# Two row tiles issued behind a memset at the start, and one query product and two sets of row statistics placed elsewhere in layer 3

## The chip, the cores and the metric

The kernel runs on one core of a Trainium2 chip. The metric is the device time of one execution in microseconds (us), as the median over runs. The engines are TensorE (PE; its weight loads are listed as PEld), VectorE (DVE), ScalarE (ACT), GpSimd (POOL) and SyncE (SP); SP, ACT and POOL can each issue DMAs.

## The reference

The input is 2048 rows (tokens) of 576 numbers. Four layers follow each other: A, B, A, B, each with a layer norm in front and a residual sum behind.

```python
def _A_ref(x, wqkv, wo):            # H = 32 heads of 18
    q, k, v = ...                   # from x @ wqkv
    phi = lambda t: jnp.where(t > 0, t + 1, jnp.exp(t)) + 1e-6
    pq, pk = phi(q), phi(k)
    kv = jnp.einsum("bhsd,bhse->bhde", pk, v)
    z = jnp.einsum("bhsd->bhd", pk)
    num = jnp.einsum("bhqd,bhde->bhqe", pq, kv)
    den = jnp.einsum("bhqd,bhd->bhq", pq, z)[..., None] + 1e-6
    o = num / den
    return (...)(o, 0, 2, 1, 3).reshape(B, S, D) @ wo

def _B_ref(x, w1, b1, w2, b2):      # 576 -> 4608 -> 576
    y = _layernorm(x, axis=-1)
    h = _gelu(jnp.einsum("bsd,df->bsf", y, w1) + b1)
    return jnp.einsum("bsf,fd->bsd", h, w2) + b2

x = x + _A_ref(_layernorm(x, axis=-1), A_wqkv, A_wo)
x = x + _B_ref(_layernorm(x, axis=-1), B_w1, B_b1, B_w2, B_b2)
x = x + _A_ref(_layernorm(x, axis=-1), A_wqkv, A_wo)
x = x + _B_ref(_layernorm(x, axis=-1), B_w1, B_b1, B_w2, B_b2)
```

(The reference calls `_B_ref` with the norm outside and inside; the kernel folds the two into one, which is why the variance step of a B layer has the form `var * (1 + eps) + eps^2`.)

## The kernel before

**Tiling.** The 2048 rows are 16 tiles of 128 (`NT`), in four column blocks of 512 tokens (`NCB`, `NCA`; `TPC` = 4 tiles each). Between layers the rows lie in DRAM (`x_d`); a layer works on `yT`, the normalised rows turned, so that features are on partitions. Weights stay on the chip. In the code layers are numbered from 0 (`li`): "layer 3" is the third one, `li == 2`, the second A layer.

**Order.** The kernel is written in a framework that records instructions in program order, derives waits from the data, and then lets a scheduler put the instructions of each engine into one fixed queue, by program order and by when they would be ready. `add_manual_dep(..., NOSYNC, ...)` adds an order between two instructions without a semaphore. TensorE's matmuls are chained one behind the other in program order (`pe`, line 138), so TensorE's order is that of the code.

**Start.** Lines 160 to 171 issue the loads: row tile 0 by SP, tiles 1 and 2 by ACT (`by_act=True`), and the others, the key, value and query weights between them, by SP in one chain. ACT's two have a manual order behind the load of the activation table (`table`). POOL meanwhile writes the identity for the transposes (a memset and an `affine_select`, lines 48 and 49), constants, a `pow` that warms up (line 55), and ones and zeros in `v_ring` (lines 183 to 185). TensorE runs nine matmuls on a zeroed tile (`warm_pe`, line 178). Tile 0 is then normalised: two `bn_stats` and an aggregate on VectorE (lines 355 to 362), the variance step (369), the `pow` on POOL (378), the normalisation on VectorE (399), five transposes on TensorE (427), copies into `yT` (430, 431), and the key product (546). Tile 1's statistics are ordered behind tile 0's variance step, its aggregate behind tile 0's normalisation.

**Layer norm pipe.** `LNPipe` takes a row tile by `feed` and moves it one stage further at each `tick`. `hold` is the number of ticks that it waits first. `stats` chooses the engine of the statistics: "dve" for `bn_stats` on VectorE, "act" for two activations with accumulators on ScalarE (lines 337 and 346) and one small step on POOL (348). `after="sum"` orders the statistics behind the latest residual sum, `after="rden"` behind the latest reciprocal denominators. `tp_at` is the row tile of the output projection from which the transposes may come.

**Output projection of an A layer.** The queries' products run in 20 pieces (`q_proj`, group of heads `g` and block `c`), kept in the list `q_left`. In layer 3 sixteen of them run between the key products (line 688), one in front of the first denominators, and two more with their phi deferred (`late`). One is left, of group 4 and block 3. The loop over `t` (line 864) then runs for each row tile `wo_stage(t)`: ten matmuls into a pair of banks (`accA` and `accB` in turn), the residual sum on VectorE (line 524), and the store; for the first four row tiles it feeds the pipe of the following layer. Between them stand, for the next block, `den_stage` (denominators), `quarter_stage` (broadcasts of their reciprocals, copied by ScalarE, line 812), `quarter_scale` (line 818) and `scale_stage` (line 797), which scale the queries on VectorE, and `quad_stage` (line 779). The rest of `q_left` is taken at `t` of 0 and 2, behind all that (line 885). The pipe ticks twice per row tile up to `t` of 9, then once.

All products other than the projection's use four banks in turn (`ps_h`, tag "h").

## Time and profile before

| | us |
|---|---|
| median of 3 runs (lowest to highest) | 764.54 (764.22 to 764.82) |
| profiled execution | 764.51 |
| its span, first to last instruction | 762.8 |
| ACT busy in the span | 336.1 |
| VectorE busy in the span | 271.5 |
| longest groups of TensorE: second product of the B layers (L1013) | 274.8 |
| first product of the B layers (L955, four groups) | 434.0 summed |

The busy times of one engine's groups can overlap, since matmuls are pipelined. The mean granted TensorE clock is given as 1.000. The stages follow one another in the span like this: the first A layer up to 105 us, the first B layer up to 387, layer 3 up to 478, and the last B layer to the end. Lines of the timeline and of the chain of waits begin with start and length in us; in the timeline they go on with engine, line, operation, what is written from what, the shape and the count, and in brackets the idle time before and what ended it. The chain is followed back from the last instruction: each piece is what released the next one.

### The profile page before, as it was taken

Reading aid. Unit: us, or ns where it says so; the run is one execution under the profiler, and the core shown is the slowest. Engines: PE = TensorE matmul, PEld = TensorE weight load, DVE = VectorE, ACT = ScalarE, POOL = GpSimd, SP = SyncE. Lnnn points to the kernel's source line nnn. Section 1 sums busy time; section 2 is a strip of 40 time slices with the busy share of each in tenths; the row PEclk is TensorE's granted clock in tenths of the full one; section 3 lists DMA queues with packets and bytes.
Section 4 is the critical chain, followed back from the end, with each engine's and each line's share of the span. In section 5 each row is a group of like instructions: output and inputs, shape, how many; then the busy total and the mean of one; then the engine's idle time right before and its main releaser. Section 6 shows DMA issues by size and latency. Waiting matters only on the chain.

```text
span 762.8 us, 15788 instructions
## 1 busy us (share of the span) xinstructions
PE 757.0 (99%) x6594; PEld 491.0 (64%) x6594; DVE 271.5 (36%) x684; ACT 336.1 (44%) x750; POOL 125.3 (16%) x198
## 2 busy tenths in 40 slices
PE   8999999999999999999999999999999999999998
PEld 5777664675477457646777767447745754674476
DVE  7786963136023503401355678600240032000000
ACT  5888857204610750264056567560164037205600
POOL 4681241002000301200110005300020021001000
PEclk9999999999999999999999999999999999999999
DMA  9991483016402721330256007530240033011000
GB/s 281 271 282 47 160 277 82 16 48 187 100 25 74 182 72 45 100 79 11 69 133 199 1 22 258 188 83 16 69 110 28 16 126 82 9 32 56 1 9 24
DMA packets 80289, 73.82 MB, mean 97 GB/s; under 512 B 36698, under 2 KB 64858, under 8 KB 80218
## 3 DMA queue, kind: packets, MB, share of 16 engines
q1 hardware_dynamic: 79930, 72.53, 32.3%
q8 instruction: 51, 0.84, 0.5%
q10 hardware_dynamic: 288, 0.30, 0.1%
q14 instruction: 20, 0.16, 0.1%
HBM read 48.03 MB, written 24.77 MB: 95 GB/s over the span
## 4 chain that ended last, share of the span: by engine, by line
PE 97%; DVE 2%; DMA 0%; issue 0%; ACT 0%; ACTq 0%
PE m_ps L1013 36%; PE h_ps L955 20%; PE hp_ps L955 16%; PE q_ps L594 6%; PE wo_ps L828 4%; PE k_ps L546 3%; PE k_ps L618 3%; PE k_ps L635 2%; PE v_ps L567 1%; PE m_half L1013 1%; PE v_ps L564 1%; PE tp L427 1%; PE kvacc L588 1%; PE k_tail L635 1%; DVE xo L524 0%; DMA x<-in_A_x_dram 0%
## 5 line engine op out<-in xcount | busy, mean ns | idle before, releaser
L1013 PE MATMUL m_ps<-w_sb,hT 128*128 128x288 bf16 x2232 | 274.8, 286 | 0.0
L1013 PEld LDWEIGHTS <-hT 128*128 128x128 bf16 x2304 | 224.8, 98 | 59.8 <-issue 3.4
L955 PEld LDWEIGHTS <-w_sb 64*128 64x128 bf16 x2304 | 124.5, 94 | 136.5 <-issue 1.9
L955 PE MATMUL hp_ps<-yT,w_sb 64*128 64x512 bf16 x1152 | 178.0, 376 | 0.0
L955 PE MATMUL h_ps<-yT,w_sb 64*128 64x512 bf16 x1152 | 147.9, 376 | 0.0
L960 ACT COPY relay_sb<-relay_sb 128x1 f32<-128x1 f32 x144 | 28.6, 198 | 259.8 <-PE h_ps L955 217.6
L951 ACT ACTIVATE hT<-h_ps,b1T 128x512 bf16<-128x512 f32 x144 | 91.2, 684 | 44.4 <-PE h_ps L955 44.4
L378 POOL TENSOR_TENSOR ln_rstd<-ln_u,neg_half 128x1 f32<-128x1 f32 x64 | 36.1, 566 | 407.0 <-DVE ln_u L369 227.2
L951 ACT ACTIVATE hT<-hp_ps,b1T 128x512 bf16<-128x512 f32 x144 | 91.2, 693 | 0.0
L524 DVE TENSOR_TENSOR xbf<-m_ps,xo 128x576 bf16<-128x576 f32 x15 | 11.4, 758 | 214.1 <-PE m_ps L1013 214.1
L524 DVE TENSOR_TENSOR xo<-m_ps,xo 128x576 f32<-128x576 f32 x16 | 12.1, 758 | 174.9 <-PE m_ps L1013 174.9
L507 POOL TENSOR_TENSOR xo<-xo,b_bc 128x576 f32<-128x576 f32 x32 | 40.7, 1277 | 100.3 <-DMA xo<-x_d 60.1
L955 PE MATMUL h_ps<-yT,w_tail 64*128 64x512 bf16 x144 | 54.1, 376 | 0.0
L955 PE MATMUL hp_ps<-yT,w_tail 64*128 64x512 bf16 x144 | 54.1, 376 | 0.0
L594 PE MATMUL q_ps<-yT,wqkv_sb 128*126 128x512 bf16 (+1 forms) x200 | 49.7, 381 | 0.0
L828 PE MATMUL wo_ps<-kvwo,pq 126*128 126x288 bf16 (+1 forms) x320 | 44.0, 286 | 0.5 <-DVE xo L524 0.3
L955 PEld LDWEIGHTS <-w_tail 64*128 64x128 bf16 x288 | 27.1, 94 | 17.1
L828 PEld LDWEIGHTS <-pq 126*128 126x128 bf16 (+1 forms) x320 | 29.7, 97 | 10.2 <-DVE pq L797 0.9
L471 ACT ACTIVATE phi_e<-k_ps 128x288 bf16<-128x288 f32 x46 | 19.3, 419 | 38.2 <-PE k_ps L618 35.8
L594 PEld LDWEIGHTS <-wqkv_sb 128*126 128x126 bf16 (+1 forms) x200 | 24.8, 131 | 11.6
L471 ACT ACTIVATE phi_e<-q_ps 126x512 bf16<-126x512 f32 (+1 forms) x40 | 23.9, 597 | 17.4 <-PE q_ps L594 17.4
L479 DVE TENSOR_SCALAR phi_e<-phi_e 128x288 bf16<-128x288 bf16 (+2 forms) x86 | 24.7, 287 | 19.1 <-ACT phi_e L471 18.4
(140 smaller groups left out, 655.6 us busy)
## 6 DMA issues: line engine op xcount, KB each, us to landing
xo<-x_d SPq DMA_DIRECT2D x48, 288.0 KB
x_d<-xo SPq DMA_DIRECT2D x32, 288.0 KB
xl<-x_d SPq DMA_DIRECT2D x24, 288.0 KB
y_d<-turned SPq DMA_DIRECT2D x40, 144.0 KB
w_sb<-in_B_w_dram SPq DMA_DIRECT2D x6, 864.0 KB
yT<-y_d SPq DMA_DIRECT2D x10, 512.0 KB
w_sb<-in_B_w_dram SPq DMA_DIRECT2D x9, 512.0 KB
x_d<-xn SPq DMA_DIRECT2D x16, 288.0 KB
```

Of the source, the lines that this page charges most:

```text
L378: nc.gpsimd.tensor_tensor(out=rstd[:], in0=it["u"][:], in1=neg_half[:], op=ALU.pow)
L471: exp = nc.scalar.activation(out=e_out, in_=ps_ap, func=ACT.Exp)
L479: low = nc.vector.tensor_scalar(out=e[0:rows, 0:n], in0=e[0:rows, 0:n], scalar1=1.0, scalar2=1e-6, op0=ALU.min, op1=ALU.add)
L507: nc.gpsimd.tensor_tensor(out=xo[:], in0=xo[:], in1=b2_bc[:], op=ALU.add)
L524: total = nc.vector.tensor_tensor(out=xn[:, cols].rearrange("p (h n) -> p h n", h=2), in0=halves, in1=xo[:, cols].rearrange("p (h n) -> p ...
L594: pe(nc.tensor.matmul(qp[0:GR[g], :], lhsT=wqkv_sb[:, k, GO[g]:GO[g] + GR[g]], rhs=yT[:, k, c * CA:(c + 1) * CA], start=(k == 0), stop=(k ...
L635: pe(nc.tensor.matmul(dst, lhsT=lhsT, rhs=pk, start=(t == 0), stop=(t == NT - 1)))
L828: pe(nc.tensor.matmul(wp[:, half, 0:HALF], lhsT=pq[(g, c)][0:GR[g], j * P:(j + 1) * P], rhs=kvwo[g][0:GR[g], half * HALF:(half + 1) * HALF ...
L951: act_last["gelu"] = nc.scalar.activation(out=to, in_=ps, func=ACT.Gelu_apprx_tanh, bias=b1T[:, f:f + 1], scale=1.0).ins.name
L955: mm = pe(nc.tensor.matmul(dst[n], lhsT=wt, rhs=mv, start=(seen[n] == 0), stop=(seen[n] == 8)))
L960: relay = nc.scalar.copy(out=relay_sb[:, 1:2], in_=relay_sb[:, 0:1])
L1013: pe(nc.tensor.matmul(acc[half][:, 0:HALF], lhsT=hT[f][:, j * P:(j + 1) * P], rhs=w2_sb[:, f, half * HALF:(half + 1) * HALF], start=(f == ...
```

## The change

Three things. At the start, tile 1's buffer gets a memset of one column by POOL, ordered behind the identity's `affine_select`; ACT's DMA of tile 1 writes the same buffer and so has to wait for it; tile 2's DMA is ordered behind tile 1's, and the order behind the table load is gone. In layer 3, the last query product is taken in front of `wo_stage(0)` and no longer behind it. And the statistics of that layer's first four new row tiles, which feed the last layer, are given out anew: tile 0 on VectorE and tile 1 on ScalarE as before, tile 2 on ScalarE and tile 3 on VectorE (they had it the other way round), with `hold` 6 and 8 where it was 2 and 4. For the first layer (`li == 0`) the expressions give what they gave.

```diff
-        nc.gpsimd.affine_select(out=ident[:], in_=ident[:], compare_op=ALU.not_equal, fill=1.0,
+        ident_done = nc.gpsimd.affine_select(out=ident[:], in_=ident[:], compare_op=ALU.not_equal, fill=1.0,
                                 base=0, pattern=[[-1, P]], channel_multiplier=1)
...
             if by_act:
+                if t == 1:
+                    tag = nc.gpsimd.memset(x0[:, 0:1], 0.0)
+                    tc.add_manual_dep(tag.ins, ident_done.ins.name, NOSYNC, reason="second rows behind the first")
                 load = nc.scalar.dma_start(out=x0[:], in_=x_in[t * P:(t + 1) * P, :])
-                tc.add_manual_dep(load.ins, table.ins.name, NOSYNC, reason="table first")
+                if t == 2:
+                    tc.add_manual_dep(load.ins, chain["act"], NOSYNC, reason="start-up DMA issue order")
+                chain["act"] = load.ins.name
...
-        table = nc.scalar.preload_act_table_set("natural_log_exp_and_others")
+        nc.scalar.preload_act_table_set("natural_log_exp_and_others")
...
                 if xn is not None and next_kind == "B" and t < TPC:
-                    lnp.feed(xn, t, "B", "pool", "act", hold=(2, 2, 2, 4)[t] if li > 0 else (2, 8, 8, 10)[t], tp_at=6 + 2 * t if li > 0 else (6, 10, 11, 14)[t],
-                             **(dict(after="sum") if t % 2 == 0 else dict(stats="act", after="rden")))
+                    lnp.feed(xn, t, "B", "pool", "act", hold=(2, 2, 6, 8)[t] if li > 0 else (2, 8, 8, 10)[t], tp_at=6 + 2 * t if li > 0 else (6, 10, 11, 14)[t],
+                             **(dict(after="sum") if t in (0, 3 if li > 0 else 2) else dict(stats="act", after="rden")))
...
+                if li > 0 and t == 0 and q_left:
+                    q_proj(*q_left.pop(0))
                 wo_stage(t)
```

## The prediction

> **What bounds the kernel now.** I read the page's busy table first, then the chain of waits for the start and for the stretch from 440 to 482 us, then the timeline of the same stretches, TensorE alone where I counted steps.

> ```profile
> span 762.8 us, 15788 instructions
> PE 757.0 (99%) x6594; PEld 491.0 (64%) x6594; DVE 271.5 (36%) x684; ACT 336.1 (44%) x750; POOL 125.3 (16%) x198
> ```

> TensorE is busy for 99% of the span: the change can win only what TensorE loses in the two places it touches. The first is the start, from the timeline:

> ```profile
> 0.80 0.39 SPq L151 DMA_DIRECT2D x<-in_A_x_dram  x1
> 0.82 0.87 ACTq L148 DMA_DIRECT2D x<-in_A_x_dram  x2
> ...
> 1.41 0.29 POOL L49 TENSOR_SCALAR_AFFINE_SELECT ident<-ident 128x128 bf16<-128x128 bf16 x1
> 1.68 0.56 POOL L55 TENSOR_TENSOR pow_warm<-pow_warm,neg_half 128x1 f32<-128x1 f32 x1
> 2.19 0.12 POOL L185 MEMSET v_ring<- 128x5 bf16 x1
> ...
> 3.66 0.46 DVE L355 BATCH_NORM_STATS2 ln_st<-x 128x6 f32<-128x288 bf16 x1 [0.72 <-DMA x<-in_A_x_dram]
> 4.83 0.45 DVE L355 BATCH_NORM_STATS2 ln_st<-x 128x6 f32<-128x288 bf16 x1
> 5.58 0.43 DVE L399 TENSOR_SCALAR y_ring<-x,ln_mv,ln_rstd 128x576 bf16<-128x576 bf16 x1
> ```

> Row tile 0 (SyncE) and tiles 1 and 2 (ScalarE) are issued together. Tile 0's statistics start at 3.66, as soon as it lands; tile 1's follow at 4.83, and tile 0's normalisation stands behind them on VectorE, at 5.58. The chain of waits runs through all three, on to the first key product at 6.98, and from 8 us on is TensorE alone. The second place is the output projection of layer 3 (chain of waits):

> ```profile
> 450.65 1.61 DVE pq L797 x4
> ...
> 452.30 0.91 PE wo_ps L828 x6
> 453.22 1.09 PE q_ps L594 x5
> ...
> 460.71 0.33 DVE quad_rden L779
> 461.05 0.37 DVE ln_st L355
> 461.42 0.37 DVE ln_st L356
> ...
> 462.13 0.76 DVE xo L524
> ...
> 464.33 0.68 DVE xo L524
> 465.01 0.04 issue
> 465.05 1.39 PE wo_ps L828 x10
> ```

> From 455.4 to 465.05 the chain is VectorE's, not TensorE's: that engine is late there, and row tile 2's statistics (461.05) are among what it does meanwhile. TensorE's own timeline shows two of the places where this is paid:

> ```profile
> 459.51 1.51 PE L828 MATMUL wo_ps<-kvwo,pq 126*128 126x288 bf16 x10
> 461.11 0.39 PE L792 MATMUL rden_ps<-quad_rden,head_bc 128*128 128x512 bf16 x1
> 464.30 0.44 PE L427 MATMUL tp<-ident,y_ring 128*128 128x128 bf16 x5
> ```

> A projection row is ten matmuls 0.122 us apart, 1.22 to 1.24 us, and 1.33 where a product of another shape follows. **Stalls**: row 0 starts at 451.45 and takes 1.60 (0.37 for the scaled queries of 450.65); row 4 starts at 459.51 and takes 1.60 (0.27, for the scaled queries of group 4 and for the quad_rden of 460.71); the five transposes of 464.30, 0.055 apart, would be through at 464.58, and row 7 starts at 465.05 (0.47, for the sum of 464.33 that frees its bank). Together 1.11; counting every product of 451.05 to 477.78 at its undisturbed step gives 25.3 of 26.73, so at most some 1.4 us can be won in layer 3.

> **Part 1, the last query product ahead of row 0.** Nothing is added: the five matmuls (1.08 us) of 453.06 (453.22 in the chain, which counts from row 0's last end) run at 451.45. Their bank is there: of the four shared banks, the two deferred query products and the direct broadcast of 450.74 hold three, and the fourth came free when the copies of 448.93 ended, at 450.5. The product now covers the wait for the scaled queries, which end at 452.26: row 0 runs from 452.53 to 453.75, row 1 to about 455.0, 0.4 earlier. Not all of it lasts. The bank of the moved product is given back only when ScalarE has done its two passes, which stand behind four others from 452.09 on; without the 0.19 idle at 454.34 they end at 455.2 for 455.41, and the broadcasts behind row 1 need that bank. VectorE's work between 451.57 and 456.53 loses 0.25 and 0.17 of idle time but waits again for row 0's later sum (453.95 for 453.25); step by step I get row 1's sum done at 456.35 for 456.53. I take **0.18** of the 0.37; the ends are 0 and 0.37. From there VectorE is dense, so the 0.27 at row 4 stays.

> **Part 2, the statistics of rows 2 and 3 exchanged, and held longer.** Row 2's two passes, their aggregate and the variance step occupy VectorE from 461.05 to 462.13, 1.08 us right behind quad_rden. They go to ScalarE: two activations with accumulator reads, 0.68 + 0.19 + 0.78 + 0.19, in the place that row 3's had from 463.70. Then row 4's sum starts at 461.0, the scalings of the next block are bound by the broadcast copies (end 462.43 before, 462.25 now), and row 5's sum is over by 464.1. Row 7 may start at 464.40, the transposes' end with part 1's 0.18: **0.47** won. Ends: 0, if the order of VectorE's queue puts other work into the gap, and 0.74, if row 4's 0.27 goes too.
> What comes back: row 3's statistics, the same 1.08 on VectorE, now behind row 7's sum. There VectorE stood idle 0.86 before 468.19, and later 0.54, 0.42, 0.76 and 0.53, so it costs nothing; with that cover gone it would be late for row 8's sum, on which row 10 waits only from 469.7. Row 3's transposes stand at 473.71 and its rows were ready at 469.57; some 1.5 us later still hides. Row 2's transposes stand at 470.96 (470.3 then); by row 3's old pace, 463.70 to 469.57, it is ready in time, and POOL has one normalisation less in front of it.

> **Part 3, the start.** One POOL memset is added, 0.10 to 0.12 by its neighbours, in a POOL idle time of 2.68 ahead of 4.99. ScalarE's two DMAs now wait for it; behind them ScalarE has the next work at 6.45 after 4.37 idle, and the table load (0.79, 1.28 long) is hidden whichever side of them it takes. SyncE's issues keep their order, with the weights now ahead of tiles 1 and 2. Gain: tile 0 shares the DMA engines with nothing but its successors in the same queue. The trace's packet records show its first packets at 1.81 (up to 0.70 long), tile 1's from 2.31, tile 0's last end marker at 3.29 and its landing at 3.64. Alone, the slowest engine would need 1.88 + 0.70 + 7 x 0.051 = 2.94, 0.35 earlier; but the first packets are slow without any neighbour, so the gain lies between 0 and 0.35; I take 0.2.
> Loss: the memset comes right behind the select (ends 1.8) or behind the pow as well (2.3), and the issue with it. Tile 1 took 3.0 from issue to landing (0.82 to 3.82), of which 1.49 up to its first packet; SyncE's first DMA needed 1.01 for that, so 2.5 to 3.0. It lands at 4.35 to 4.85, or at 4.85 to 5.35. Its statistics start then, and tile 0's normalisation 0.75 after that, against 5.58: no loss up to a landing at 4.81, 0.54 at 5.35. Averaged over the two orders the start **loses 0.1**; ends: 0.35 won, 0.54 lost. Tile 2 lands about 1.3 later than the 5.58 of before, below the 7.33 at which it is read. The key weights land at 6.33 and 6.64 and are read from 6.98: a gain of over 0.5 would stop there.
> [...]

> **The sum.** 762.8 of span and 1.7 around it are the profiled execution's 764.51, 0.03 under the median of 764.54. 764.51 - 0.18 - 0.47 + 0.1 = **764.0**. From about 478 us on both traces should be the same, shifted.

> **Rivals.**
> Everything goes: VectorE, 1.08 ahead, also covers row 4, and tile 1 lands before 4.81. 1.11 to 1.4 in layer 3 and 0.2 to 0.35 at the start: 762.8 to 763.2. For it: VectorE is the only late engine from 455 to 465. Against: row 4's stall comes before the statistics that leave. Chance 0.22.
> The wait moves: the engines' queues are ordered by a list scheduler, and with the statistics gone the broadcast copies on ScalarE (2.05 us for each block) become the late ones, or row 0's later sum eats the 0.18. Then layer 3 gives 0 to 0.3, and with the start's 0.1 the time is 764.3 to 764.6. For it: ScalarE's copies end only 0.4 before the scalings that read them. Against: VectorE's chain has hardly a gap. Chance 0.18.
> Slower: the second row tile lands like the third did. That one took 4.33 (issue 1.25, landing 5.58), since it shared the engines with the key weights all the way. Issued at 1.85 to 2.35 behind those weights, tile 1 would land at 6.2 to 6.7, tile 0's normalisation, queued behind its statistics, would start at 6.95 to 7.45, 1.37 to 1.87 late, and nothing later gets that back, as the chain is TensorE from there. With the 0.65 of layer 3: 765.2 to 765.7. It decides from a landing at 5.46 on (0.65 lost). For it: the weights are issued from 1.24 on, ahead of tile 1. Against: tile 1 itself, in the same competition, took 3.0. Chance 0.17.

> **The numbers.** The forecast (763.4 to 764.3) has the remaining 0.43. Range 762.9 to 765.3: it takes in the first two rivals nearly whole and the slower one's nearer end. A measurement of this kernel tells no change from one of about 0.2%, 1.53 us. Faster by more needs a time under 763.0: most of the first rival, and a little of the forecast if two of its terms are at their ends, 0.2. Slower by more needs over 766.07: the slower rival without any gain in layer 3, 0.06. Within: 0.74.

> **What would show it.** Right: the product of 453.06 directly behind den_pair, and row 0 in ten even steps; no bn_stats on VectorE between rows 3 and 6; no wait ahead of row 7; 0.5 to 0.8 less from 451.05 to the first h_ps matmul. For part 3: tile 0's statistics start before 3.66, tile 1's between 4.5 and 5.4, the first key product near 6.98. Wrong: a wait of TensorE for a bank ahead of the moved product or of the first broadcasts; the first key product beyond 7.5; or VectorE taking tile 0's normalisation ahead of tile 1's statistics, so that TensorE waits at tile 1's transposes (7.60) instead.

## The result and the profile after

| | before | after |
|---|---|---|
| median of 6 runs (lowest to highest), us | 764.68 (764.22 to 765.79) | 769.07 (766.75 to 769.76) |
| profiled execution's span | 762.8 | 768.0 |

The ratio is 1.0054, 95% interval 1.0043 to 1.0065: the changed kernel is 4.4 us slower, where 0.5 less was forecast and 765.3 was the upper end of the range. The page of the changed kernel begins like this (its second line gives busy time and share of the span for each engine; the third is the granted TensorE clock in 40 slices, in tenths):

```profile
span 768.0 us, 15786 instructions
...
PE 759.5 (99%) x6594; PEld 492.6 (64%) x6594; DVE 271.2 (35%) x684; ACT 336.7 (44%) x750; POOL 126.0 (16%) x199
...
PEclk8999999999999999999999999999999999999999
```

The clock's digit is below 9 in the first slice alone, so the place to look is the start. The shift of TensorE's instructions says the same; "shift" is how much later (or, negative, earlier) one of them starts than in the profile of before. There the two that matter at the start stood like this (start, length, engine, line, operation):

```profile
6.98 0.79 PE L546 MATMUL k_ps<-wqkv_sb,yT 128*128 128x288 bf16 x5
7.60 0.44 PE L427 MATMUL tp<-ident,y_ring 128*128 128x128 bf16 x5
```

In the changed kernel the first key product is 0.47 earlier (6.51), tile 1's transposes are 3.50 later (11.10), tile 2's 5.85 later, and from 20 us to the beginning of layer 3's projection everything is 5.64 later. Behind that projection it is 5.22 later: the rest of the change gave 0.42 back. The timeline of the start, changed kernel (start, length, engine, line, operation; in brackets the idle time before and what ended it; the lines of the code have moved by 5 against before):

```profile
2.19 0.10 POOL L149 MEMSET x<- 128x1 bf16 x1
...
2.32 0.89 ACTq L151 DMA_DIRECT2D x<-in_A_x_dram  x2
...
3.03 0.46 DVE L360 BATCH_NORM_STATS2 ln_st<-x 128x6 f32<-128x288 bf16 x1
...
4.95 0.43 DVE L404 TENSOR_SCALAR y_ring<-x,ln_mv,ln_rstd 128x576 bf16<-128x576 bf16 x1 [0.67 <-POOL ln_rstd L383]
...
6.51 0.79 PE L551 MATMUL k_ps<-wqkv_sb,yT 128*128 128x288 bf16 x5
6.65 0.46 DVE L360 BATCH_NORM_STATS2 ln_st<-x 128x6 f32<-128x288 bf16 x1 [0.18 <-DMA x<-in_A_x_dram]
...
9.01 0.46 DVE L360 BATCH_NORM_STATS2 ln_st<-x 128x6 f32<-128x288 bf16 x1 [1.54 <-DMA x<-in_A_x_dram]
9.39 0.19 DVE L367 BATCH_NORM_AGGREGATE ln_mv<-ln_st 128x2 f32<-128x12 f32 x1
...
10.62 0.43 DVE L404 TENSOR_SCALAR y_ring<-x,ln_mv,ln_rstd 128x576 bf16<-128x576 bf16 x1 [0.66 <-POOL ln_rstd L383]
...
11.10 0.71 PE L432 MATMUL tp<-ident,y_ring 128*128 128x128 bf16 x5 [3.81 <-DVE y_ring L404]
```

Read it from the top. The memset comes behind the warm-up pow, and ScalarE issues tile 1 at 2.32 for 0.82 before. Tile 0 does land earlier, 3.00 for 3.64. Tile 0's normalisation (4.95) no longer stands behind tile 1's statistics: the scheduler has put it first. Tile 1 lands at 6.63, and its statistics start at once. Then VectorE waits 1.54 us: the instruction at 9.01 is the first half of **tile 2's** statistics, which stands in VectorE's queue ahead of tile 1's aggregate (9.39), and tile 2 lands at 8.99. Only then come tile 1's aggregate, its normalisation (10.62) and its transposes, for which TensorE has waited 3.81 us.

What follows runs at half the granted clock, as the table of windows shows (window, its length, busy time and count of PE, PEld, DVE, ACT and POOL, granted clock, DMA share, GB/s):

```profile
6.00:8.00 2.00, 1.29 (x9) 0.49 (x6) 1.11 (x3) 0.87 (x2) 0.00 (x0) 1.00 1.08 348
8.00:10.00 2.00, 0.00 (x0) 0.00 (x0) 0.94 (x4) 0.00 (x0) 0.00 (x0) 0.85 1.09 330
10.00:12.00 2.00, 0.90 (x7) 0.81 (x8) 0.57 (x2) 0.36 (x1) 0.55 (x1) 0.50 1.06 316
12.00:14.00 2.00, 2.00 (x10) 1.21 (x9) 0.69 (x5) 0.85 (x3) 1.26 (x3) 0.50 1.03 277
14.00:16.00 2.00, 2.00 (x10) 1.36 (x9) 1.14 (x5) 1.13 (x3) 0.43 (x1) 0.50 0.93 267
16.00:18.00 2.00, 2.00 (x20) 1.60 (x18) 1.47 (x6) 0.85 (x2) 0.00 (x0) 0.94 0.87 258
```

The trace's clock records give the edges: full from 6.01, half from 9.42 to 16.25, then full up to 767.18, in a span of 768.0. In that time five transposes take 0.51 instead of 0.28, fifteen key products 3.60 instead of 1.99, and five value products 1.05 instead of 0.54: 2.35 us together. So 3.50 of lateness and 2.35 of half clock make 5.85, and 0.21 that TensorE waited at the first key-value sums (`kvacc`, 13.83 to 14.29 in the kernel before) is gone: **5.64**.

Layer 3 (chain of waits, changed kernel; start and length) has kept its one stretch on VectorE, but a shorter one, ahead of row 4's end instead of row 7:

```profile
463.20 0.61 DVE xo L529
...
463.88 1.42 DVE pq L823 x4
465.30 0.33 DVE pq L802
465.63 0.67 DVE xo L529
466.30 0.34 DVE quad_rden L784
466.64 0.04 issue
466.68 0.39 PE rden_ps L797
```

### The profile page after: what moved, and what is told of

Same layout as the page of the kernel before. It is cut to its first block, busy times and chain, and to the rows that moved or that the text cites. A ratio compares the mean times of both kernels' runs of the same rounds, so it can differ in the third digit from the quotient of the medians.

```text
span 768.0 us, 15786 instructions
## 1 busy us (share of the span) xinstructions
PE 759.5 (99%) x6594; PEld 492.6 (64%) x6594; DVE 271.2 (35%) x684; ACT 336.7 (44%) x750; POOL 126.0 (16%) x199
## 4 chain that ended last, share of the span: by engine, by line
PE 98%; DMA 1%; DVE 1%; POOL 0%; issue 0%; ACTq 0%; POOLq 0%
PE m_ps L1020 36%; PE h_ps L962 20%; PE hp_ps L962 16%; PE q_ps L599 6%; PE wo_ps L833 5%; PE k_ps L551 3%; PE k_ps L623 3%; PE k_ps L640 2%; PE v_ps L572 1%; PE v_ps L569 1%; PE m_half L1020 1%; PE tp L432 1%; DMA x<-in_A_x_dram 1%; PE kvacc L593 1%; PE k_tail L640 1%; PE rden_ps L797 0%
```

## The experiments

Each kernel ran in up to 5 rounds beside the kernel before, on the same chip. Diffs are against the changed kernel where nothing else is said.

**The start alone, and layer 3 alone.** The first undoes the layer 3 parts, the second the start.

```diff
# start_only
-                    lnp.feed(xn, t, "B", "pool", "act", hold=(2, 2, 6, 8)[t] if li > 0 else ...
+                    lnp.feed(xn, t, "B", "pool", "act", hold=(2, 2, 2, 4)[t] if li > 0 else ...
-                             **(dict(after="sum") if t in (0, 3 if li > 0 else 2) else ...
+                             **(dict(after="sum") if t % 2 == 0 else ...
-                if li > 0 and t == 0 and q_left:
-                    q_proj(*q_left.pop(0))
```

> Only the start of the change (memset, ScalarE's two DMAs behind it, no order behind the table load); layer 3 as before. Theory (the start alone costs 5.64 us in the changed profile, layer 3 gives 0.42 back): 5.6 us slower than before where the clock is lost at the start, about 2.9 to 3.3 where it is kept; the median near 769.3, ratio near 1.006. Rival (the three parts act on one another, or layer 3 costs something too): within 1 us of before.

Measured 769.84 (768.70 to 770.37), before 764.55, ratio 1.0054 (1.0040 to 1.0068); shift 5.86 from 23 us to the end. Tile 2 landed at 10.21 in this execution and held tile 1's transposes up to 12.33.

> Only the two parts in layer 3 (query product ahead of row 0, statistics of rows 2 and 3 exchanged and held longer); start as before. Theory: 0.42 us faster than before, 764.2 to 764.3, as the changed profile's shift falls from 5.64 to 5.22 in layer 3. Rival (that fall comes from the other phase of the start): no difference, 764.7. My prediction had 0.65.

Measured 764.12, before 764.55, ratio 0.9993 (0.9985 to 1.0002). Its profile has a shift of -0.03 ahead of the projection and -0.47 behind it, so 0.43 won, the same as in the changed kernel; the times alone agree but their interval reaches past 1. The whole loss is the start's.

**Which part of the start.** One argument orders tile 2's statistics behind tile 1's normalisation.

```diff
# order
-        feed0(2, after=dve_last["turned"])
+        feed0(2, after=dve_last["norm"])
```

> The changed kernel, but row tile 2's statistics ordered behind row tile 1's normalisation on VectorE (one argument of the feed). Theory (tile 1's aggregate stood behind tile 2's first bn_stats, which waited 1.54 us for tile 2's landing at 8.97): tile 1's transposes at 9.1 instead of 11.1, 2.0 us won in waiting, and TensorE's idle stretch falls from 3.8 to 1.8 us, so that the clock may be kept, worth up to 2.4 more: 764.8 to 767.2. Rival (the late landing of tile 1 at 6.63 is the whole price and the order costs nothing): as the changed kernel, 769.

Measured 765.19 (764.92 to 765.98), before 764.55, ratio 1.0004 (0.9996 to 1.0013), with a granted clock of 1.000. The timelines of VectorE and of TensorE in that kernel:

```profile
7.30 0.21 DVE L367 BATCH_NORM_AGGREGATE ln_mv<-ln_st 128x2 f32<-128x12 f32 x1
...
8.36 0.43 DVE L404 TENSOR_SCALAR y_ring<-x,ln_mv,ln_rstd 128x576 bf16<-128x576 bf16 x1 [0.66 <-POOL ln_rstd L383]
9.02 0.46 DVE L360 BATCH_NORM_STATS2 ln_st<-x 128x6 f32<-128x288 bf16 x1 [0.23 <-DMA x<-in_A_x_dram]
```

```profile
8.84 0.45 PE L432 MATMUL tp<-ident,y_ring 128*128 128x128 bf16 x5 [1.66 <-DVE y_ring L404]
```

Tile 1 landed at 6.42, not much earlier than in the changed kernel (6.63), and tile 2 at 9.00. Yet tile 1's transposes come 2.26 earlier than in the changed kernel (some 0.2 of it by the landing), the wait is 1.66, and the clock stays. Of the shift of 5.64, only 1.35 is left: the late landing alone costs that much, the order in VectorE's queue and the clock it lost made the rest.

**The clock by itself.** Twelve matmuls that compute nothing that is used fill part of the wait:

```diff
# fill
                     if li == 0 and t == 0 and half == 0:
+                        warm_pe(12)
                         lnp.tick()
```

> The changed kernel with 12 idle-filling matmuls on the zeroed tile ahead of row tile 1's transposes (2.6 us at full clock, in the 3.8 us in which TensorE waits). They compute nothing that is used. Theory (the idle stretch costs the clock, and half the clock from 11.1 to 16.2 costs 2.4 us): granted clock 1.000 from 6 us on in every run, 2.4 us less than the changed kernel's profile, 766.6 to 767.3, and the runs no longer spread over 3 us. Rival (the clock goes for another reason, or its loss is hidden behind late loads): 769 as before the filling.

Measured 766.97 (766.78 to 767.49), before 764.55, ratio 1.0023 (1.0014 to 1.0032). The windows of that kernel, columns as above:

```profile
8.00:10.00 2.00, 1.72 (x8) 0.59 (x6) 0.94 (x4) 0.00 (x0) 0.33 (x1) 1.00 1.08 324
10.00:12.00 2.00, 1.26 (x13) 0.99 (x14) 1.03 (x5) 0.88 (x3) 0.31 (x2) 1.00 1.10 321
```

Tile 1's transposes stand at 10.74, nearly as late as in the changed kernel, but the clock is full and the shift is 2.79 instead of 5.64. Of the 2.85 between the two, 0.36 is there already at the transposes (tile 2 landed at 8.62 here); the rest, 2.49, is close to the 2.35 that the half clock had cost. The median is 2.1 below the changed kernel's, and the runs lie within 0.7 us of each other instead of 3.0. So the idle stretch is what cost the clock here: 0.50 was granted to the matmuls behind the 3.81 of idle TensorE, 1.00 to those here.

**Why tile 1 lands late.** The memset loses its order behind the identity's select:

```diff
# early
                     tag = nc.gpsimd.memset(x0[:, 0:1], 0.0)
-                    tc.add_manual_dep(tag.ins, ident_done.ins.name, NOSYNC, reason="second rows behind the first")
```

> The changed kernel without the order of the memset behind the identity's select, so that POOL runs it at about 1.05 and ScalarE issues row tile 1 at about 1.15, ahead of SyncE's key weights at 1.24. Theory (a DMA is served behind the large transfers that were issued before it, whichever queue it is in): tile 1 lands at 3.9 to 4.4, tile 0 at 3.0 to 3.6, no wait at tile 1's transposes, and only layer 3's gain is left: 764.0 to 764.3. Rival (waiting for the memset as such, or the two queues' sharing, delays tile 1): landing above 5.5 and 766 or more.

Measured **763.73** (763.49 to 764.17), before 764.60, ratio 0.9979 (0.9970 to 0.9988): faster than both kernels. The timeline:

```profile
1.04 0.10 POOL L149 MEMSET x<- 128x1 bf16 x1
...
1.17 0.93 ACTq L150 DMA_DIRECT2D x<-in_A_x_dram  x2
...
1.23 0.42 SPq L160 DMA_DIRECT2D wqkv_sb<-in_A_wqkv_dram  x1
...
3.12 0.46 DVE L359 BATCH_NORM_STATS2 ln_st<-x 128x6 f32<-128x288 bf16 x1 [0.19 <-DMA x<-in_A_x_dram]
...
4.31 0.46 DVE L359 BATCH_NORM_STATS2 ln_st<-x 128x6 f32<-128x288 bf16 x1
...
6.93 0.77 PE L550 MATMUL k_ps<-wqkv_sb,yT 128*128 128x288 bf16 x5 [0.20 <-DMA wqkv_sb<-in_A_wqkv_dram]
```

The same wait for the same memset, but issued 0.06 ahead of the key weights instead of 1.08 behind them: tile 1 lands at 4.16, 2.98 after its issue, as before (3.00), for 4.31 in the changed kernel. There the packet records show its first packet at 4.72, among the end markers of the key weights' two transfers (issued at 1.24 and 1.71), which come from 4.33 to 5.63. Tile 0 still lands early (3.10), and VectorE's queue has its old order. What now limits the start are the key weights, at 6.89 in this execution, so its shift at 20 us is only -0.07. In the profiles of early_hold and early_hold2 below, which have the same start, the weights land at 6.07 and 5.78 and the shift is -0.45 and -0.41; so I read the early kernel's median, 0.39 below that of layer 3 alone.

**Tile 1 by SyncE, directly behind tile 0.**

```diff
# sp_second
-                if t == 1:
+                if t == 2:
                     tag = nc.gpsimd.memset(x0[:, 0:1], 0.0)
...
-        load_x0(1, by_act=True)
+        load_x0(1)
```

> The changed kernel with row tile 1 issued by SyncE right behind tile 0, ahead of the key weights; the memset and ScalarE's DMA are left for tile 2. Theory: tile 0 alone on the engines lands at 3.0 to 3.1 and tile 1 at about 3.5, the key weights some 0.4 later than in the changed kernel, at 6.2 and 6.5, so that the first key product starts at 6.4 to 6.6 for 6.98 before and nothing waits behind it: 0.4 to 0.6 at the start and 0.43 in layer 3, 763.5 to 763.9, faster than both. Rival (the weights then land too late, or tile 2, at 6.4 to 7, delays what follows): no better than layer 3's part alone, 764.1 or more.

Measured 764.22 (763.27 to 764.90), before 764.60, ratio 0.9985 (0.9976 to 0.9994). The profiled execution is also the fastest one of this kernel (763.27). In it tile 0 lands at 2.96, tile 1 at 3.44, the weights at 6.34 and 6.57, and the shift is -0.82 already at 20 us. But it is a gain only when the weights come in time: in the execution profiled for sp_hold, below, which has this start, they land at 6.79 and after, and TensorE waits for them:

```profile
6.83 0.65 PE L548 MATMUL k_ps<-wqkv_sb,yT 128*128 128x288 bf16 x4 [0.49 <-DMA wqkv_sb<-in_A_wqkv_dram]
```

**Layer 3, the two parts apart**, each alone on the kernel before.

```diff
# query_only, against before
+                if li > 0 and t == 0 and q_left:
+                    q_proj(*q_left.pop(0))
                 wo_stage(t)
# stats_only, against before: hold=(2, 2, 6, 8)[t] and "t in (0, 3 if li > 0 else 2)" alone
```

> Only the last query product of layer 3 moved ahead of row 0; the statistics and the start as before. Theory (row 0's stall of 0.37 is covered, and the 0.28 that comes back at row 4 has to do with the moved product's late bank or phi): the first row of the projection 0.35 earlier against the start of the stage, less or nothing left behind row 4, the wait of 0.47 ahead of row 7 stays: 764.3 to 764.6. Rival (the 0.28 at row 4 comes from the exchanged statistics): 0.35 kept to the end, 764.2.

> Only the statistics of rows 2 and 3 of layer 3 exchanged and held longer; the query product and the start as before. Theory (VectorE was late for row 5's sum because of row 2's statistics): the wait of 0.47 ahead of row 7 goes, nothing else moves, 764.1. Rival (the 0.28 lost at row 4 in the changed kernel is from this part): 0.2 won, 764.35.

Query product alone: 764.47 for 764.60, ratio 0.9992 (0.9983 to 1.0001). Statistics alone: 764.16 for 764.60, ratio 0.9986 (0.9977 to 0.9995). TensorE's timelines, first of the query product alone, then of the statistics alone (whose profiled execution is 1.4 us late from the start on, so only lengths and waits are to be compared):

```profile
459.14 1.79 PE L828 MATMUL wo_ps<-kvwo,pq 126*128 126x288 bf16 x10
461.02 0.39 PE L792 MATMUL rden_ps<-quad_rden,head_bc 128*128 128x512 bf16 x1
...
464.97 1.27 PE L828 MATMUL wo_ps<-kvwo,pq 126*128 126x288 bf16 x9 [0.31 <-DVE xo L524]
```

```profile
453.70 0.91 PE L828 MATMUL wo_ps<-kvwo,pq 72*128 72x288 bf16 x6 [0.19 <-DVE pq L797]
...
460.90 1.50 PE L828 MATMUL wo_ps<-kvwo,pq 126*128 126x288 bf16 x10
...
465.97 1.40 PE L828 MATMUL wo_ps<-kvwo,pq 126*128 126x288 bf16 x10
```

With the product moved, row 1 starts 0.34 earlier against the start of the stage, and row 4 takes 1.88 up to the next product where it took 1.60: 0.28 comes back, and 0.06 is left at the end. With the statistics moved, rows 0 and 4 are as before, and the 0.47 ahead of row 7 are gone (row 7 begins 0.28 after the transposes); 0.10 comes back later, ahead of row 12. So the product's theory held, its rival fell, and of the 0.43 of layer 3 the statistics bring 0.37 and the product 0.06.

**The last stall of layer 3.** Row 0's statistics were held too, on the early kernel and on the kernel with tile 1 by SyncE.

```diff
# early_hold, against early; sp_hold has the same, against sp_second
- hold=(2, 2, 6, 8)[t] if li > 0 ..., tp_at=6 + 2 * t if li > 0 ...
+ hold=(6, 2, 6, 8)[t] if li > 0 ..., tp_at=(8, 9, 10, 12)[t] if li > 0 ...
# early_hold2
+ hold=(6, 2, 6, 8)[t] if li > 0 ..., tp_at=(8, 6, 10, 12)[t] if li > 0 ...
```

> The early kernel (memset at the front of POOL's work), with row 0's statistics in layer 3 held for 6 ticks instead of 2, so that on VectorE they stand behind the quad_rden product, where row 2's stood before the change, and the transposes of rows 0 and 1 let in from row tiles 8 and 9 of the projection. Theory (VectorE is full from the first row to the quad_rden product, and row 0's statistics, 1.1 us, are the last thing in there that can wait): the stall at row 4 goes, 0.25 to 0.37 more than in the early kernel, 763.4 to 763.5 against its 763.73. Rival (the statistics there make row 5's sum late again, as row 2's did): no gain, the wait ahead of row 7 is back, 763.7 to 764.1.

> The same hold in layer 3 on the kernel in which SyncE issues row tile 1 right behind tile 0. Theory: as much faster than sp_second's 764.22 as early_hold is than early, 763.8 to 764.0, with the same spread of the runs, since the spread comes from the start. Rival (the spread of sp_second was chance): median near its best run less 0.3, 763.0 to 763.3.

767.03 and 767.96 for 764.53; ratios 1.0027 (1.0017 to 1.0036) and 1.0036 (1.0022 to 1.0049). A miss, by a wait of my own making, and the two kernels do not compute row tile 1 of the last layer: row 3's normalisation gets the buffer of the ring of three (`y_ring`) that row 1 still stands in, so TensorE waits for it (it runs on POOL from 469.38 to 470.87) and turns row 3's values in the place of row 1's. Their times say only what such a wait costs (early_hold, TensorE):

```profile
470.92 0.53 PE L431 MATMUL tp<-ident,y_ring 128*128 128x128 bf16 x5 [2.41 <-POOL y_ring L399]
```

In sp_hold's profiled execution the same wait, 2.42, also cost the clock: its records show half from 472.76 to 476.17, and the shift grows there from 2.25 to 3.90.

> As early_hold (row 0's statistics held for 6 ticks), but row 1's transposes stand in the projection from row tile 6 and row 0's from 8, so that row 3's normalisation finds its slot of the ring of three already read. In early_hold and sp_hold it took the slot of row 1 before row 1 was transposed, so those two compute row tile 1 of the last layer from row tile 3's values, and TensorE waited 2.7 us for them. Theory (VectorE's fullness ahead of row 4 was the last stall of that stage): row 4 without a stall, row 7 without a wait, no new wait; 0.3 to 0.4 less than early's 763.73, so 763.3 to 763.5, 1.1 faster than before. Rival (the transposes or another row come late instead): 763.7 or more.

764.78 for 764.51, ratio 0.9998 (0.9989 to 1.0007). Row 4 takes 1.50 where it took 1.88 in early, and the shift falls from -0.42 at the start of the stage to -0.87 behind row 4 and to -1.34 at row 7, as expected; then VectorE waits for the residual rows of the last four row tiles:

```profile
474.41 0.76 DVE L528 TENSOR_TENSOR xo<-wo_ps,xo 128x576 f32<-128x576 f32 x1 [1.72 <-DMA xo<-x_d]
```

Those loads were issued late (SyncE's fourth from last of this layer at 470.97, for 467.51 in early). The chain of waits (early_hold2; start and length) shows what it waited for, a store of finished rows:

```profile
465.80 5.15 DMA x_d<-xo
470.96 0.02 issue
470.97 0.32 SPq L504
```

In early the same store was issued 1.60 earlier, at 464.20, and landed 3.29 later, at 467.49. Ahead of it in SyncE's queue stands a load that here waits 2.8 for POOL and goes at 465.39 (463.79 in early), as row 0's normalisation ends at 465.36: the row tiles share nine buffers, and row 0's is in use until 4.9 us later than in early, which fits the 1.60; which buffer the load takes is argued from the code. Why the store then took 5.15 is not shown. The gain of 0.92 up to row 7 (0.54 in early) turns into a loss of 1.6 behind row 12. The early kernel remains the fastest.

## Why the prediction was wrong, point by point

**Part 1 (0.18 forecast): 0.06.** The stall at row 0 went as forecast, and so did the idea that VectorE would give most of it back. The size is off because VectorE's chain won only 0.1 (quad_rden at 460.53 for 460.64 in the layer 3 kernel).

**Part 2 (0.47 forecast): 0.47, less 0.10 that a later row gives back.** Right, by the mechanism stated; that nothing would come back was not.

**Part 3 (0.1 lost forecast): 5.64 lost in the profile, 5.29 in the median of start_only.** Here the prediction failed, in three of its steps.

The step "2.5 to 3.0 from issue to landing" took tile 1's own earlier path, in which nothing large had been issued ahead of it. Behind the key weights it took 4.31. The rival named this, with tile 2's row as its price, and its landing of 6.2 to 6.7 holds the measured 6.63. I gave it 0.17 because tile 1 had taken 3.0 "in the same competition", but it was not the same: there it was issued ahead of the weights (0.82 for 1.24). The same holds for tile 2, which I had at 6.9 and which landed at 8.99.

The step "Its statistics start then, and tile 0's normalisation 0.75 after that" assumed VectorE's old order, and so did the rival: its price of 1.37 to 1.87 was for a late normalisation of tile 0, which in fact came 0.63 early (4.95 for 5.58). My list of signs had the other order, tile 0's normalisation ahead, but only as a wait at tile 1's transposes; that tile 2's statistics would slip in front of tile 1's aggregate, and so bind tile 1 to the landing of tile 2, I did not see. It is about 2.0 of tile 1's lateness, by the order kernel (2.26, less 0.21 by which tile 1 landed earlier there).

```profile
6.01:9.42 3.41, 1.28 (x9) 0.48 (x6) 1.52 (x5) 0.86 (x2) 0.00 (x0) 1.00 1.08 337
```

```profile
469.35:472.76 3.41, 1.15 (x12) 0.92 (x13) 1.50 (x4) 1.98 (x3) 2.24 (x4) 1.00 0.43 156
```

```profile
5.18:8.59 3.41, 1.82 (x13) 0.80 (x12) 1.31 (x4) 0.89 (x2) 0.00 (x0) 1.00 1.05 315
```

After the first two the clock fell, though TensorE had been busy for 1.28 and 1.15 of them; after the third, with 1.82, it stayed. By that estimate, whether a wait costs the clock depends also on where the periods lie, and their start differs from run to run: the first full clock begins anywhere from 4.14 (fill) to 9.61 (stats_only) in these profiles. This is how I read the changed kernel's spread: 766.75 with a mean granted clock of 1.000, 768.5 to 768.6 with 0.997, 769.5 to 769.8 with 0.995, which would be no period, one and two at half clock; of these, the two of a run with 0.995 (769.74, the profiled one) are in the records.

**Tile 0's gain** was 0.63 instead of 0.2 (landing 3.00 for 3.64), more than the 0.35 that I held possible: its slow first packets were shorter, 0.37 at most instead of 0.70, with ScalarE's DMAs issued later (2.32 for 0.82). Why they were shorter is not shown.

## What to carry to other kernels

Delaying a small load to protect another can put it behind a large transfer issued meanwhile: place it by what is issued ahead of it, not by the microseconds of the delay (1.5 us later in issue was 2.8 later in landing). When an input comes later, look at the order in each engine's queue again, because the scheduler can put that input's first instruction in front of work that is ready earlier (here tile 2's, with a wait of 1.54, in front of tile 1's aggregate). And a long wait of TensorE can cost twice, once as idle time and once in clock: here waits of 3.81 (the changed kernel) and 2.42 (sp_hold) did, those of 2.41 (early_hold) and 1.66 (order) did not, by the profiled executions, and 12 matmuls of filling brought 2.1 us back in the median.

## What the runs showed of the hardware that was not expected

The kernel before has two starts of its own. On one chip 20 of its 32 runs lay between 764.4 and 765.1 and 12 between 765.9 and 766.2. The profile of the statistics kernel (765.53, where most of its runs are near 764.1) shows the later start: its first transposes begin at the same time but take 0.51 instead of 0.29, the first five key products 1.20 instead of 0.62, and the second five transposes still take 0.53 (8.64 to 9.17). Its clock records say full from 9.61, for 5.36 in the profile of before, and it is 1.40 late to the end. None of the ten runs of the early kernel (763.5 to 764.2) and of the eleven of early_hold2 (764.4 to 765.3), which has the same start, lies so far above the others. Why is not shown: TensorE's idle time ahead of the first transposes, 0.73 in the profile of before, is 0.20 in that of early but 0.89 in that of early_hold2.
